# Block-sparse attention with an MLP mixer on one core: Q as whole rows, score products on four quarters of the array, V rows of 136 columns

## The chip, the core and the metric

The kernel runs on one core of one Trainium2 chip. A core has a matrix engine (TensorE, in the profile PE, with its weight loads as PEld), a vector engine (DVE), a scalar engine (ACT), GpSimd (POOL) and SyncE (SP), which here only issues DMAs. SBUF has 128 partitions; TensorE writes into PSUM, whose banks hold 2048 bytes in each partition. The metric is the time of one execution on the device in microseconds; lower is better.

## The reference

Two batches, eight heads, 768 queries of 64 numbers each. Every query sees the keys less than 16 positions away, and besides them 24 summary keys, one for each block of 32 keys.

```python
k_sum = k.reshape(B, H, nb, block, D).max(axis=3)
v_sum = v.reshape(B, H, nb, block, D).mean(axis=3)
mask_l = np.abs(pos[:, None] - pos[None, :]) < window
scores_s = scale * np.einsum('bhsd,bhnd->bhsn', q, k_sum) + np.log(block)
scores_all = np.concatenate([np.where(mask_l, scores_l, -1e9), scores_s], axis=-1)
a = np.exp(scores_all - scores_all.max(-1)); a = a / (a.sum(-1) + 1e-9)
attn = a @ np.concatenate([v, v_sum], axis=2)
...
u = x + tokenmix(x)               # x: attn, heads side by side, 512 columns
u = u + relu(u @ w_ch1) @ w_ch2   # 512 -> 1536 -> 512
out = u + relu(layernorm(u) @ moe2_w_ch1) @ moe2_w_ch2   # 512 -> 2048 -> 512
```

## The kernel before

The work has two parts. The attention goes pair by pair (two heads of one batch, eight pairs), and each pair in three **steps** of four windows of 64 queries: 24 steps, n = 0 to 23. Behind it, and partly beside it, stand the token mixing (`g1`, `g2`) and two large feed-forward layers, whose products are made in three parts from operands split into a high and a low half (`mm3`); the weights are loaded as 62 pieces and split on DVE and ACT (`dec`, `wh`, `wl`).

One step of the attention is a chain over the engines. `att_qk` makes the scores `sc` on PE: for each of four windows one product whose stationary side is a 128 x 128 piece of Q and whose moving side is 120 columns of K (96 neighbours and 24 summary keys). The 128 columns of the piece are the 64 queries of one head and the 64 queries of the other; since both heads' rows stand in the 128 partitions, the tile Q is filled in a pattern of blocks with zeros between, so that each query meets its own head's keys alone. `att_exp` reads the scores on DVE four times (`sn`, with the mask added and the row's extreme `mn` beside it), and ACT takes four exponentials `pr`. `att_tr` transposes the four `pr` on PE into `pt`, `att_evac` copies that to `PT` in SBUF (ACT, in every third step DVE), `att_av` multiplies with V in eight products of 64 columns of the array (`av`), `att_norm` divides on DVE (`rec`, `u`), and `att_hi` (ACT, `xh`) and `att_lo` (POOL, `xl`) split the result for the token mixing.

Per pair there are loads of K, Q (two DMAs of 64 partitions, in pieces of 512 bytes), V (two) and a transposed V (`VT`). `prep_k` and `copy_k` make the summary keys, `prep_v1` sums VT on POOL (for pair 0 on DVE, `Z`), `prep_v2` transposes Z on PE (`psv`) and ACT copies it into V four times. K and Q of three pairs fit at a time, V and VT of two.

The order of the work comes from the table `ORDER`: each event of step n or pair i gets a time (for `att_qk` it is n), `attention` sorts them and emits them, and a scheduler of the language then orders each engine's instructions. Scores lie in PSUM in the pool `ps_sc` with two buffers of one bank, so that the scores of step n can be written when the reads of step n-2 are done. Every DMA on SP waits until the DMA that was issued eight earlier has landed. Pair 0's Q is the one load that is issued from ACT's queue (`load_pair(0, nc.scalar)`). At the start, two memsets on DVE and four on POOL write the zeros of the three Q tiles, and 24 large products on PE (`warm`) run before the first load lands.

Of the kernel before, what the change touches and what calls it, by code (L numbers as in the profile page):

```python
# [26 lines left out]
NK = 96 + NB  # L27
ST = S // P
# [24 lines left out]
class Kern:  # L53
# [227 lines left out]
    def att_qk(self, n):  # L281
# [3 lines left out]
        ps = self.ps_sc.tile([P, 4, P], F32, tag="sc", name=f"sc{n}")  # L285
        for u in range(4):
            w = 4 * qd + u
            a = 184 * (w // 2) + 88 * (w % 2)
            nc.tensor.matmul(  # L289
                ps[:, u, :NK],  # L290
                Q[:, 64 + P * w : 64 + P * w + P],
                K.rearrange("p v c -> p (v c)")[:, a : a + NK],
                start=True,
                stop=True,
            )
        self.sc[n] = ps

    def att_exp(self, n):
# [7 lines left out]
        for u in range(4):  # L306
# [4 lines left out]
                ps[:, u, :NK],  # L311
# [26 lines left out]
    def att_av(self, n):  # L338
# [6 lines left out]
        for u in range(4):  # L345
            w = 4 * qd + u
            j = w % 2
            for r in range(2):
                nc.tensor.matmul(  # L349
                    ps[64 * j : 64 * j + 64, u // 2, 65 * r : 65 * r + 65],  # L350
                    pt[:, u * P + 64 * (r ^ j) : u * P + 64 * (r ^ j) + 64],
                    V[:, j, w // 2, 64 * r : 64 * r + 65],
                    start=True,
                    stop=True,
                )
# [264 lines left out]
    def run(self):  # L620
# [22 lines left out]
        self.ps_sc = actx.enter_context(tc.tile_pool(name="ps_sc", bufs=2, space=PSUM))  # L643
# [22 lines left out]
        for i in range(3):  # L666
# [183 lines left out]
```

## Time and profile before

| | |
|---|---|
| median of 3 runs | 613.52 us (613.23 to 614.16) |
| the profiled execution: its own time | 612.73 us |
| its span in the trace | 610.9 us |
| PE busy | 587.1 us (96%), 3368 instructions |
| DVE busy | 340.4 us (56%) |
| ACT busy | 208.5 us (34%) |
| mean granted clock of PE | 0.985 of full speed |

The span is the time from the first to the last instruction that the profiler recorded; the time of the same execution is 1.8 us longer, for what lies around the span. "Busy" is the time in which an engine executes anything. PE's busy time comes from records whose ends are modelled: a busy PE can be one that runs at half clock, which the row of the granted clock tells.

### The profile page before, as it was taken

Reading aid. Unit: us, or ns where it says so; the run is one execution under the profiler, and the core shown is the slowest. Engines: PE = TensorE matmul, PEld = TensorE weight load, DVE = VectorE, ACT = ScalarE, POOL = GpSimd, SP = SyncE. Lnnn points to the kernel's source line nnn. Section 1 sums busy time; section 2 is a strip of 40 time slices with the busy share of each in tenths; the row PEclk is TensorE's granted clock in tenths of the full one; section 3 lists DMA queues with packets and bytes.
Section 4 is the critical chain, followed back from the end, with each engine's and each line's share of the span. In section 5 each row is a group of like instructions: output and inputs, shape, how many; then the busy total and the mean of one; then the engine's idle time right before and its main releaser. Section 6 shows DMA issues by size and latency. Waiting matters only on the chain.

```text
span 610.9 us, 8732 instructions
## 1 busy us (share of the span) xinstructions
PE 587.1 (96%) x3368; PEld 521.6 (85%) x3368; DVE 340.4 (56%) x857; ACT 208.5 (34%) x458; POOL 45.8 (7%) x81
## 2 busy tenths in 40 slices
PE   7678899999999999999999999999999999999997
PEld 4567788879989898998989999999988999899896
DVE  5378778899567799787789951111143311111122
ACT  3677786535234345334334411111121110110110
POOL 2445433100000000000000000000000000000000
PEclk9779899999999999999999999999999999999999
DMA  9999862245423433344333200000000100000011
GB/s 213 290 228 234 212 156 75 75 133 169 142 67 113 132 89 90 102 134 125 117 104 104 69 1 1 0 1 0 1 17 36 53 0 1 1 0 1 0 53 52
DMA packets 27261, 51.78 MB, mean 85 GB/s; under 512 B 2130, under 2 KB 15186, under 8 KB 27220
## 3 DMA queue, kind: packets, MB, share of 16 engines
q1 hardware_dynamic: 26356, 50.80, 29.4%
q8 instruction: 26, 0.43, 0.3%
q10 hardware_dynamic: 864, 0.43, 0.3%
q14 instruction: 15, 0.12, 0.1%
HBM read 48.07 MB, written 3.15 MB: 84 GB/s over the span
## 4 chain that ended last, share of the span: by engine, by line
PE 88%; DVE 4%; DMA 3%; ACT 3%; issue 1%; POOL 1%; ACTq 0%; SPq 0%; DVEq 0%; POOLq 0%
PE sc L289 2%; PE av L349 2%; PE g L199 2%; PE g L198 1%; PE g L200 1%; DMA V<-in_v_dram 1%; DMA Q<-in_q_dram 1%; PE pt L326 1%; PE tx L510 1%; DVE dec L135 1%; PE tu L443 1%; ACT pr L319 1%; PE acc_('x', 2)_0_4643 L199 1%; PE acc_('x', 0)_0_3642 L199 1%; PE acc_('x', 0)_2_3644 L199 1%
## 5 line engine op out<-in xcount | busy, mean ns | idle before, releaser
L135 DVE SCALAR_TENSOR_TENSOR dec<-stage,dec 128x512 uint32<-128x512 uint32 x62 | 44.1, 712 | 0.8
L182 DVE TENSOR_TENSOR wl<-dec,wh 128x512 fp32r<-128x512 f32 x62 | 43.0, 696 | 1.2 <-DMA stage<-in_wts_dram 1.1
L131 DVE SCALAR_TENSOR_TENSOR dec<-stage,dec 128x512 uint32<-128x512 uint32 x62 | 42.9, 692 | 0.9
L113 ACT ACTIVATE dec<-stage 128x512 f32<-128x512 f32 x62 | 41.6, 673 | 4.7 <-DMA stage<-in_wts_dram 4.6
L175 ACT CAST wh<-dec 128x512 fp32r<-128x512 f32 x62 | 38.0, 616 | 12.7 <-DVE dec L135 12.5
L319 ACT ACTIVATE pr<-sn,mn 128x120 f32<-128x120 f32 x96 | 31.7, 385 | 7.6 <-DVE mn L309 7.4
L289 PE MATMUL sc<-K,Q 128*128 128x120 f32 x192 | 29.8, 304 | 1.5 <-DMA Q<-in_q_dram 1.0
L289 PEld LDWEIGHTS sc<-K,Q 128*128 128x128 f32 x192 | 26.9, 214 | 3.2 <-issue 1.4
L127 DVE TENSOR_SCALAR dec<-dec 128x512 f32<-128x512 f32 x62 | 26.5, 429 | 2.6 <-ACT dec L113 2.4
L129 DVE TENSOR_SCALAR dec<-dec 128x512 uint32<-128x512 uint32 x62 | 27.2, 439 | 0.8
L309 DVE CUSTOM_DVE_ANT_0 sn<-sc,mask 128x120 f32<-128x120 f32 x96 | 22.3, 275 | 8.8 <-PE sc L289 4.3
L326 PE MATMUL pt<-ident,pr 128*120 128x128 f32 x96 | 20.1, 294 | 6.7 <-ACT pr L319 2.8
L389 POOL TENSOR_TENSOR xl<-u,xh 128x256 fp32r<-128x256 f32 x24 | 19.7, 824 | 65.9 <-ACT xh L380 65.9
L349 PEld LDWEIGHTS av<-V,PT 121*64 121x64 f32 x384 | 16.2, 144 | 9.3 <-issue 5.8
L349 PE MATMUL av<-V,PT 121*64 121x65 f32 x384 | 19.8, 237 | 4.4 <-issue 3.8
L326 PEld LDWEIGHTS pt<-ident,pr 128*120 128x120 f32 x96 | 11.8, 142 | 10.0 <-ACT pr L319 5.0
L260 POOL TENSOR_TENSOR VT<-VT 128x384 f32<-128x384 f32 (+3 forms) x28 | 18.2, 650 | 1.6
L272 ACT ACTIVATE V<-psv 24x384 f32<-24x384 f32 x32 | 14.1, 476 | 4.9 <-PE psv L269 4.8
L199 PE MATMUL g<-xl,wh 128*128 128x256 f32 x48 | 14.5, 304 | 0.7 <-POOL xl L389 0.6
L198 PE MATMUL g<-xh,wh 128*128 128x256 f32 x48 | 14.0, 306 | 0.5 <-ACT xh L380 0.5
L200 PE MATMUL g<-xh,wl 128*128 128x256 f32 x48 | 14.0, 300 | 0.5 <-DVE wl L182 0.5
L485 DVE TENSOR_SCALAR xn<-u,mv,rs 128x128 f32<-128x128 f32 x48 | 13.9, 341 | 0.0
(3007 smaller groups left out, 1678.7 us busy)
## 6 DMA issues: line engine op xcount, KB each, us to landing
stage<-in_wts_dram SPq DMA_DIRECT2D x62, 512.0 KB, 3.5
V<-in_v_dram SPq DMA_DIRECT2D x16, 290.2 KB, 7.8
K<-in_k_dram SPq DMA_DIRECT2D x8, 480.0 KB, 8.5
VT<-in_vt_dram SPq DMA_DIRECT2D x8, 384.0 KB, 6.8
out_dram<-u SPq DMA_DIRECT2D x12, 256.0 KB, 2.0
Q<-in_q_dram SPq DMA_DIRECT2D x7, 224.0 KB, 7.9
Q<-in_q_dram SPq DMA_DIRECT2D x7, 192.0 KB, 6.9
mask<-in_mask_dram SPq DMA_DIRECT2D x1, 240.0 KB, 5.3
```

Source lines behind the costliest of these rows:

```text
L113: nc.scalar.activation(m, self.raw[n][:, :, 1].bitcast(F32), AF.Abs)
L127: nc.vector.tensor_scalar(m, m, MAG_LO, MAG_HI, op0=ALU.max, op1=ALU.min)
L129: nc.vector.tensor_scalar(mi, mi, 3, 0x3FFFFFF8, op0=ALU.logical_shift_left, op1=ALU.bitwise_and)
L131: nc.vector.scalar_tensor_tensor(mi, t[:, :, 1], 0xC0000000, mi, op0=ALU.bitwise_and, op1=ALU.bitwise_or)
L135: nc.vector.scalar_tensor_tensor(mi, t[:, :, 0], 29, mi, op0=ALU.logical_shift_right, op1=ALU.bitwise_or)
L175: self.nc.scalar.copy(self.slots[c if c < 16 else c - 16][0][:, s], x)
L182: self.nc.vector.tensor_tensor(wl[:, s], x, f32(wh[:, s]), op=ALU.subtract)
L199: nc.tensor.matmul(out, lhs[0], rhs[1], start=False, stop=False)
L289: nc.tensor.matmul(ps[:, u, :NK], Q[:, 64 + P * w : 64 + P * w + P], K.rearrange("p v c -> p (v c)")[:, a : a + NK], start=True, stop=True,)
L319: nc.scalar.activation(pr[:, u], sn[:, u], AF.Exp, bias=mn[:, u : u + 1], scale=-1.0)
L326: nc.tensor.transpose(ps[:NK, u * P : u * P + P], pr[:, u], self.ident)
L349: nc.tensor.matmul(ps[64 * j : 64 * j + 64, u // 2, 65 * r : 65 * r + 65], pt[:, u * P + 64 * (r ^ j) : u * P + 64 * (r ^ j) + 64], V[:, j ...
```

## The change

Q is kept as it comes: one tile of 128 x 768 (64 rows of each head), without zeros, filled by one DMA of whole rows of 3072 bytes. The six memsets and the padding on the host fall away. The scores of a window are now two products, one for each head r, each with a stationary side of 64 x 64 in the quarter of the array with rows 64r and columns 64(r^j), where j is the window's parity; a step has eight such products of 120 columns instead of four that fill the array. They are written to one PSUM tile `scores` of two banks, one for each j: even steps use one half of both banks, odd steps the other. `att_exp` reads it there. `att_av` emits its eight products in the order e, r, j instead of u, r, so that neighbours lie in different column halves. V's rows grow from 129 to 136 columns (3096 to 3264 bytes in a row of a DMA).

```diff
+VC = 136
...
-        qa, qb = self.q[b, p, 0:64], self.q[b, p, 64:128]
-        queue.dma_start(
-            Q[64:128, 128:1664].rearrange("p (n c) -> p n c", c=256)[:, :, 0:128],
-            qb[:, 64 : 64 + S].rearrange("p (n c) -> p n c", c=128),
-        )
-        queue.dma_start(
-            Q[0:64, :1664].rearrange("p (n c) -> p n c", c=128)[:, ::2],
-            qa.rearrange("p (n c) -> p n c", c=128),
-        )
+        queue.dma_start(Q, self.q[b, p])
...
-        ps = self.ps_sc.tile([P, 4, P], F32, tag="sc", name=f"sc{n}")
-        for u in range(4):
-            w = 4 * qd + u
-            a = 184 * (w // 2) + 88 * (w % 2)
-            nc.tensor.matmul(
-                ps[:, u, :NK],
-                Q[:, 64 + P * w : 64 + P * w + P],
-                K.rearrange("p v c -> p (v c)")[:, a : a + NK],
...
+        ps = self.scores[:, :, n % 2]
+        for e in range(2):
+            for r in range(2):
+                for j in range(2):
+                    w = 4 * qd + 2 * e + j
+                    a = 184 * (w // 2) + 88 * j
+                    rows, cols = slice(64 * r, 64 * r + 64), slice(64 * (r ^ j), 64 * (r ^ j) + 64)
+                    nc.tensor.matmul(
+                        ps[cols, j, e, :NK],
+                        Q[rows, 64 * w : 64 * w + 64],
+                        K.rearrange("p v c -> p (v c)")[rows, a : a + NK],
...
-                ps[:, u, :NK],
+                ps[:, u % 2, u // 2, :NK],
...
-        for u in range(4):
-            w = 4 * qd + u
-            j = w % 2
+        for e in range(2):
             for r in range(2):
...
+                for j in range(2):
+                    u = 2 * e + j
...
+        self.scores = ps_sc.tile([P, 2, 2, 2, P], F32, name="scores")
...
-        self.Q = [att.tile([P, 2 * S + P], F32, name=f"Q{i}") for i in range(3)]
+        self.Q = [att.tile([P, S], F32, name=f"Q{i}") for i in range(3)]
-        self.V = [att.tile([NK + 1, 2, 6, 129], F32, name=f"V{i}") for i in range(2)]
+        self.V = [att.tile([NK + 1, 2, 6, VC], F32, name=f"V{i}") for i in range(2)]
...
-        for i in range(3):
-            blocks = self.Q[i].rearrange("p (n c) -> p n c", c=P)
-            for rows, first in ((slice(0, 64), 1), (slice(64, P), 0)):
-                (nc.vector if i == 0 else nc.gpsimd).memset(blocks[rows, first::2], 0.0)
```

The scheduler orders the instructions anew. On PE, just behind the 24 `warm` products, the program of before begins with the scores of steps 0, 1 and 2 (`sc_186`, `sc_213`, `sc_236`):

```order
L289 MATMUL sc_186<-K_97,Q_94 128x120 [waits DMAHW1_49,DMAHW2_49,DMAHW0_49,Activation_49]
L289 MATMUL sc_186<-K_97,Q_94 128x120 x3
L289 MATMUL sc_213<-K_97,Q_94 128x120 x4
L269 MATMUL psv_218<-ident,Z_106 120x128 [waits DMAHW4_49,DVE_49,Pool_49]
L326 MATMUL pt_245<-ident,pr_204 120x128 [waits Activation_49] x2
L289 MATMUL sc_236<-K_97,Q_94 128x120 [waits DVE_49]
L289 MATMUL sc_236<-K_97,Q_94 128x120 x3
L326 MATMUL pt_245<-ident,pr_204 120x128 [waits Activation_49] x2
L349 MATMUL av_285<-V_102,PT_100 64x65 [waits DMAHW0_49,DMAHW6_49,Activation_49,Pool_49]
```

After the change all steps write the one tile `scores`:

```order
L285 MATMUL scores<-K_98,Q_95 64x120 [waits DMAHW1_49,DMAHW0_49,Activation_49]
L285 MATMUL scores<-K_98,Q_95 64x120 x7
L262 MATMUL psv_216<-ident,Z_107 120x128 [waits DMAHW3_49,DVE_49,Pool_49]
L322 MATMUL pt_246<-ident,pr_199 120x128 [waits Activation_49]
L285 MATMUL scores<-K_98,Q_95 64x120 [waits DVE_49]
L285 MATMUL scores<-K_98,Q_95 64x120 x7
L322 MATMUL pt_246<-ident,pr_199 120x128 [waits Activation_49] x3
L285 MATMUL scores<-K_98,Q_95 64x120 [waits DVE_49]
L285 MATMUL scores<-K_98,Q_95 64x120 x7
L345 MATMUL av_289<-V_103,PT_101 64x65 [waits DMAHW5_49,DMAHW7_49,Activation_49,Pool_49]
```

The scores of step 1 (the second group of `scores`) stood before without a wait, right behind those of step 0; now they wait for DVE, and stand behind the transpose `psv` and the first transpose of step 0. The product `av` of step 0 stands behind the scores of step 2 in both.

On ACT, the same place in the program: `pr_204` (before) and `pr_199` (after) are the exponentials of step 0, the next two `pr` those of steps 1 and 2, `V` the copies of `psv`, `PT` the copy of step 0's transposes.

```order
L244 COPY K_97<-ks_182 128x7x24 [waits DVE_49]
L319 ACTIVATE pr_204<-sn_202,mn_203 128x120 [waits DVE_49] x4
L272 ACTIVATE V_102<-psv_218 24x6x64 [waits PE_49]
L272 ACTIVATE V_102<-psv_218 24x6x64 x3
L319 ACTIVATE pr_227<-sn_225,mn_226 128x120 [waits DVE_49] x4
L319 ACTIVATE pr_259<-sn_257,mn_258 128x120 [waits DVE_49] x4
L336 COPY PT_100<-pt_245 120x512 [waits PE_49]
L244 COPY K_98<-ks_200 128x7x24 [waits DVE_49]
L380 CAST xh_112<-u 128x2x128 [waits DVE_49]
```

```order
L237 COPY K_98<-ks_175 128x7x24 [waits DVE_49]
L265 ACTIVATE V_103<-psv_216 24x6x64 [waits PE_49]
L315 ACTIVATE pr_199<-sn_197,mn_198 128x120 [waits DVE_49] x4
L265 ACTIVATE V_103<-psv_216 24x6x64 x3
L315 ACTIVATE pr_225<-sn_223,mn_224 128x120 [waits DVE_49] x4
L332 COPY PT_101<-pt_246 120x512 [waits PE_49]
L315 ACTIVATE pr_260<-sn_258,mn_259 128x120 [waits DVE_49] x4
L376 CAST xh_113<-u 128x2x128 [waits DVE_49]
L237 COPY K_99<-ks_195 128x7x24 [waits DVE_49]
```

The copy `PT` of step 0 stood behind twelve exponentials and four copies into V; now it stands behind eight and four. One copy into V has moved ahead of step 0's exponentials.

On SP, the loads of pair 1 (`K_98`, `Q_95` before; `K_99`, `Q_96` after) and what stands ahead of them:

```order
L228 DMA V_102<-in_v_dram 96x774
L684 DMA V_102<-in_guard_dram 1x1548 [waits DMAHW0_49]
L684 DMA V_103<-in_guard_dram 1x1548 [waits DMAHW1_49]
L208 DMA K_98<-in_k_dram 128x6x160 [waits DMAHW2_49]
L210 DMA Q_95<-in_q_dram 64x6x128 [waits DMAHW3_49]
L214 DMA Q_95<-in_q_dram 64x7x128 [waits DMAHW4_49]
L686 DMA gt<-in_g_dram 128x4 [waits DMAHW5_49]
L221 DMA VT_105<-in_vt_dram 128x768 [waits DMAHW6_49]
```

```order
L221 DMA V_103<-in_v_dram 96x816
L676 DMA V_103<-in_guard_dram 1x1632
L676 DMA V_104<-in_guard_dram 1x1632 [waits DMAHW0_49]
L209 DMA K_99<-in_k_dram 128x6x160 [waits DMAHW1_49]
L210 DMA Q_96<-in_q_dram 128x768 [waits DMAHW2_49]
L678 DMA gt<-in_g_dram 128x4 [waits DMAHW3_49]
L214 DMA VT_106<-in_vt_dram 128x768 [waits DMAHW4_49]
```

With one DMA less ahead of it, each load waits for a landing that lies one earlier in the row: the load of K of pair 1 waits on DMAHW1 instead of DMAHW2, and only one DMA of V's last row, instead of two, waits at all. Behind the last event of the attention the two programs stand in the same order on every engine.

## Rows read from the trace of the kernel before

**Rows 1.** The page, part 2: PE's busy share and granted clock in 40 slices.
```profile
PE   7678899999999999999999999999999999999997
...
PEclk9779899999999999999999999999999999999999
```

**Rows 2.** Busy time by stretch: columns stand in the first line.
```profile
core 0: us, PE busy (x) PEld busy (x) DVE busy (x) ACT busy (x) POOL busy (x), PEclk, DMA share, GB/s
9.80:31.30 21.50, 13.92 (x122) 12.28 (x123) 10.70 (x60) 14.88 (x43) 6.69 (x14) 0.84 1.08 270
31.30:82.00 50.70, 42.18 (x411) 36.26 (x410) 42.16 (x164) 37.46 (x98) 25.52 (x41) 0.90 0.93 226
82.00:113.00 31.00, 30.92 (x309) 26.38 (x310) 25.19 (x95) 21.89 (x61) 7.84 (x10) 1.00 0.34 96
113.00:165.00 52.00, 50.48 (x262) 44.34 (x261) 46.36 (x90) 23.81 (x44) 1.19 (x2) 1.00 0.44 138
...
15.34:22.17 6.83, 4.89 (x33) 4.80 (x34) 1.51 (x10) 3.65 (x12) 2.27 (x3) 0.50 1.06 287
...
225.00:611.00 386.00, 382.25 (x1942) 344.18 (x1940) 168.07 (x364) 86.42 (x169) 0.00 (x0) 1.00 0.14 44
```

**Rows 3.** The timeline of 0 to 20 us, all engines: start, length, instruction.
```profile
9.79 0.95 DVE L252 TENSOR_REDUCE Z<-VT 128x24 f32<-128x768 f32 x1 [3.47 <-DMA VT<-in_vt_dram]
9.79 2.02 PE L289 MATMUL sc<-K,Q 128*128 128x120 f32 x16 [0.98 <-DMA Q<-in_q_dram]
...
10.95 0.28 DVE L309 CUSTOM_DVE_ANT_0 sn<-sc,mask 128x120 f32<-128x120 f32 x1
...
11.28 1.26 ACT L319 ACTIVATE pr<-sn,mn 128x120 f32<-128x120 f32 x4 [4.59 <-DVE mn L309]
...
12.44 1.72 ACT L272 ACTIVATE V<-psv 24x384 f32<-24x384 f32 x4
...
14.18 2.39 ACT L319 ACTIVATE pr<-sn,mn 128x120 f32<-128x120 f32 x8
...
16.59 0.59 ACT L336 COPY PT<-pt 120x512 f32<-120x512 f32 x1
...
17.28 1.23 PE L349 MATMUL av<-V,PT 121*64 121x65 f32 x16 [3.83 <-issue]
...
19.77 0.72 POOL L389 TENSOR_TENSOR xl<-u,xh 128x256 fp32r<-128x256 f32 x1 [14.38 <-ACT xh L380]
```

**Rows 4.** Waits of DVE, 31.3 to 113 us: total, times, longest.
```profile
DVE rec L363 <- PE av L349: 4.2, 5, 1.1
DVE sn L309 <- PE sc L289: 2.9, 2, 2.4
```

**Rows 5.** Busy time by stretch, as above: two stretches of saturated DMA.
```profile
25.00:27.00 2.00, 1.90 (x24) 1.42 (x24) 1.36 (x11) 1.95 (x7) 1.12 (x5) 1.00 1.02 400
29.00:31.00 2.00, 0.46 (x4) 0.47 (x5) 0.00 (x0) 1.96 (x7) 0.00 (x0) 1.00 1.27 178
```

**Rows 6.** The chain in order of time, 0 to 108 us: start, length, step.
```profile
23.48 0.34 PE psv L269
...
43.12 1.77 PE sc L289 x8
...
94.55 0.88 PE sc L289 x8
...
95.77 0.38 PE av L349 x4
...
98.61 0.67 PE av L349 x16
...
100.36 0.44 PE pt L326 x4
```

**Rows 7.** The timeline of 82 to 89 us: one step's scores and reads.
```profile
84.10 1.05 PE L289 MATMUL sc<-K,Q 128*128 128x120 f32 x8
...
85.29 0.27 DVE L309 CUSTOM_DVE_ANT_0 sn<-sc,mask 128x120 f32<-128x120 f32 x1
```

More of the change, by code (lines that the diff above doesn't have):

```diff
@@ L284, in att_qk @@
         Q, K = self.Q[i % 3], self.K[i % 3]
-        ps = self.ps_sc.tile([P, 4, P], F32, tag="sc", name=f"sc{n}")
-        for u in range(4):
-            w = 4 * qd + u
-            a = 184 * (w // 2) + 88 * (w % 2)
-            nc.tensor.matmul(
-                ps[:, u, :NK],
-                Q[:, 64 + P * w : 64 + P * w + P],
-                K.rearrange("p v c -> p (v c)")[:, a : a + NK],
-                start=True,
-                stop=True,
-            )
+        ps = self.scores[:, :, n % 2]
[9 more added lines that the diff above has]
+                        K.rearrange("p v c -> p (v c)")[rows, a : a + NK],
+                        start=True,
+                        stop=True,
+                    )
         self.sc[n] = ps
@@ L344, in att_av @@
         self.av[n] = ps
-        for u in range(4):
-            w = 4 * qd + u
-            j = w % 2
+        for e in range(2):
             for r in range(2):
[L349 to L355, printed above, removed]
+                for j in range(2):
+                    u = 2 * e + j
+                    nc.tensor.matmul(
+                        ps[64 * j : 64 * j + 64, e, 65 * r : 65 * r + 65],
+                        pt[:, u * P + 64 * (r ^ j) : u * P + 64 * (r ^ j) + 64],
+                        V[:, j, 2 * qd + e, 64 * r : 64 * r + 65],
+                        start=True,
+                        stop=True,
+                    )
     def att_norm(self, n):
@@ L642, in run @@
         self.ps_mm = ctx.enter_context(tc.tile_pool(name="ps_mm", bufs=2, space=PSUM))
-        self.ps_sc = actx.enter_context(tc.tile_pool(name="ps_sc", bufs=2, space=PSUM))
+        ps_sc = actx.enter_context(tc.tile_pool(name="ps_sc", bufs=1, space=PSUM))
+        self.scores = ps_sc.tile([P, 2, 2, 2, P], F32, name="scores")
         self.ps_pt = actx.enter_context(tc.tile_pool(name="ps_pt", bufs=2, space=PSUM))
@@ L665, in run @@
         nc.gpsimd.memset(warm[1], 0.0)
-        for i in range(3):
-            blocks = self.Q[i].rearrange("p (n c) -> p n c", c=P)
-            for rows, first in ((slice(0, 64), 1), (slice(64, P), 0)):
-                (nc.vector if i == 0 else nc.gpsimd).memset(blocks[rows, first::2], 0.0)
-            if i == 0:
-                for t in self.Z:
-                    nc.gpsimd.memset(t, 0.0)
-                for t in self.V:
-                    nc.gpsimd.memset(t[0:NB, 0, :, 64:65], 1.0)
-                    nc.gpsimd.memset(t[96:NK, 1, :, 64:65], 1.0)
+        for t in self.Z:
+            nc.gpsimd.memset(t, 0.0)
+        for t in self.V:
+            nc.gpsimd.memset(t[0:NB, 0, :, 64:65], 1.0)
+            nc.gpsimd.memset(t[96:NK, 1, :, 64:65], 1.0)
         for t in self.PT:
@@ L792, in _layout @@
     t = lambda x: x.reshape(B, NPAIR, 2, S, D)
-    a["q"] = np.zeros((B, NPAIR, P, S + P), np.float32)
-    a["q"][..., 64 : 64 + S] = t(q).transpose(0, 1, 2, 4, 3).reshape(B, NPAIR, P, S)
+    a["q"] = t(q).transpose(0, 1, 2, 4, 3).reshape(B, NPAIR, P, S)
     a["vt"] = t(v).transpose(0, 1, 2, 4, 3).reshape(B, NPAIR, P, S)
@@ L800, in _layout @@
     vp[:, :, :, 16 : 16 + S] = t(v)
-    vw = np.ones((B, NPAIR, 2, 96, 6, 129), np.float32)
+    vw = np.ones((B, NPAIR, 2, 96, 6, VC), np.float32)
     for w in range(NW):
@@ L822, in _layout @@
     a["mask"] = _mask()
-    a["guard"] = np.zeros((1, 2, 6, 129), np.float32)
+    a["guard"] = np.zeros((1, 2, 6, VC), np.float32)
     a["guard"][..., 64] = EPS
```

## The prediction

> **What bounds the kernel now.** I read first the 40 slices of the page [rows 1]: PE stands at 9 tenths or more from slice 5 to the last but one, at full clock; only the first five slices (0 to 76 us) show gaps, and the lower clocks lie there too. Then busy time by stretch [rows 2], which cuts the attention into three regimes:
>
> - 9.8 to 31.3 us, the start: no engine is full (PE 13.92 and ACT 14.88 of 21.50), the DMA engines are (share 1.08). What counts is the chain of single waits.
> - 31.3 to 82 us: PE and DVE are both busy 42.2 of 50.7, ACT 37.5. They take turns at waiting.
> - 82 to 113 us: PE is busy 30.92 of 31.00. PE alone sets the end.
>
> Behind that, from 113 to 165 PE is busy 50.48 of 52.00, and from 225 to 611 it is 382.25 of 386.00. No edit touches those instructions, and their order is the same in both programs, so the time changes by as much as the attention ends earlier or later.
>
> **The first step of the chain.** In the timeline [rows 3] the scores of steps 0 and 1 (16 records) start at 9.79, the sums `Z` of VT at the same 9.79; the first read `sn` follows at 10.95, behind Z and its copy. ACT takes four exponentials (11.28), four copies into V (12.44), eight exponentials (14.18, steps 1 and 2), and only then, at 16.59, the copy `PT` of step 0 on which `av` (17.28) waits. From `av` hang `xl` on POOL (19.77), behind it POOL's sums for pair 1, and `psv` at 23.48 [rows 6]. So here ACT's order sets what comes later.
>
> **What the change costs and saves, part by part.**
>
> *ACT's order at the start.* PT of step 0 now stands behind eight exponentials instead of twelve. Eight took 2.39 [rows 3], so four are 1.20 us. Against it one copy into V, 1.72 / 4 = 0.43 us, now stands ahead of the first exponentials. It waits for `psv`, which waits for Z (done at 10.95), so it may push the exponentials back: between 0 and 0.6 us. Together the order gives -0.6 to -1.2; I take -0.9.
>
> *Q's load.* A stretch in which mostly Q's 512-byte pieces move shows 178 GB/s, one in which K, V and weights move 400, both at full DMA share [rows 5]. Q is 0.39 MB a pair: at 178 GB/s 2.2 us, at 400 1.0 us. So up to 1.2 us of DMA time per pair. Q of pair 0 stands ahead of the load of VT that releases Z at 9.79, and the DMA engines share the time between both, so not all arrives there: bounds 0 and -1.2. The K of pair 1 is also issued a landing earlier. I take -1.2 in all, since Z, the scores and the later loads of the start all stand behind the same full DMA engines. Behind 31.3 us I book nothing: no wait of DVE on a load stands in its list [rows 4], and the work of the three engines covers the loads; if that cover is not complete, what shows is a gain again, not a loss.
>
> Start: -0.9 - 1.2 = **-2.1** (from -0.5 to -2.5).
>
> *The scores on quarters.* Before, a step's scores are 8 records in 0.88 us, 0.110 each [rows 6]. Now there are 16 of the same 120 columns. No row shows 64 x 64. The nearest is `av`: 121 x 64, two column halves. There 16 records take 0.67 us and 4 take 0.38 [rows 6], which makes 0.29 / 12 = 0.024 a record and 0.28 fixed per visit. At the rate of the scores, 0.110 / 120 per column, a record of 65 columns would be 0.060, and 16 in a row 0.95. So `av` does run two halves or more side by side, and pays 0.28 for entering and leaving. Bounds for the new scores: four at once without any fixed part 0.44; one after another with it 16 x 0.110 + 0.28 = 2.04; two at once 0.88 + 0.28 = 1.16; four at once with the fixed part 0.44 + 0.28 = **0.72**. I take the last, because it is nearest to what `av` shows, where records of different quarters overlap: -0.16 us a step at full clock. At half clock (8 records in 1.77 [rows 6]) it is 0.88 + 0.28 to 0.56, that is -0.33 to -0.61.
>
> The Trainium skill, "TensorEngine Tiling (Array Packing)", Key Properties, says that a change of tiling mode drains the array, and that tiles operate independently; the program has such changes in 93 places instead of 51. The fixed 0.28 in [rows 6] agrees with a drain, and it is in the sum already.
>
> *One buffer pair instead of two buffers.* This is the loss. Both steps' halves share both banks, so the scores of step n+1 now wait for the reads of step n, where they waited for those of n-1 (the order at the start shows it: the second group of scores has a wait on DVE that it had not). [Rows 7] show a place where this bites: scores start at 84.10, and the last read of the step before starts at 85.29 and takes 0.27, so these scores would be 1.46 late. Behind them on PE stand transposes and an `av`, and DVE's next reads wait for them. The order has been made anew and puts other PE work ahead of many scores, so that most of the wait is filled. The reads of one step follow those of the step before mostly after 1 us or more, which covers a score block of 0.72. Bounds: 0, and 1.46 in each of the six steps of the PE-bound stretch, 8.8 us. I take +0.6 once between 31.3 and 82, and +0.3 in all between 82 and 113.
>
> *31.3 to 82.* DVE waits for scores only twice, 2.9 us, the longer 2.4 us [rows 4]; that is a score block at half clock on the chain at 43.12 [rows 6]. It gets 0.5 shorter (the middle of 0.33 and 0.61). With the +0.6: **+0.1** (from -1.5 to +2).
>
> *82 to 113.* Six steps of 0.16 = -1.0, plus 0.3: **-0.7** (from -1.5 to +8).
>
> *The rest.* The order of `av`'s products: `av` overlaps already; bounds -0.1 and +0.1 a step, I take 0. V's 5.4% more bytes are 31 KB a pair, 0.08 us at 400 GB/s and 0.17 at 178, hidden where loads land early, 0. The memsets of Q (DVE and POOL) lie ahead of 9.79, while the first loads are on their way, 0.
>
> **Sum.** -2.1 + 0.1 - 0.7 = **-2.7 us**. The profiled execution took 612.73 (span 610.9 and 1.8 around it) and would take 610.0. The median of the runs shown, 613.52, lies 0.8 above it; I take the change from there: **610.8**. Its own range is 608 to 612.3.
>
> **The rivals.**
>
> *More at the start (R1).* From 15.34 to 22.17 PE runs at half clock (0.50) and is busy 4.89 of 6.83 [rows 2]. It follows a stretch in which PE idles (3.83 us ahead of 17.28 [rows 3]). If `av` comes 2 us earlier, this gap is halved, and the slow stretch may not come or come shorter: half of the 4.89, some 2.4 us, comes back on top of the sum, or up to 4 with the half-clock blocks near 43 us. For it: the gap is the longest of the start. Against it: scores and `av` still wait for each other, and three gaps remain. Time 605 to 608; from there down to 603 at best.
>
> *No change (R2).* DVE and ACT carry 42.2 and 37.5 of 50.7 us in the middle stretch [rows 2], with the same number of instructions as before. What the start gains can run out against them: a chain that is 2 us early meets a DVE that has 8.5 us of idle time in all, 7 of them behind PE [rows 4]. Then only the -0.7 is left, and the new waits take it back: 612.5 to 614.5.
>
> *Quarters that do not run four at once (R4).* Two row halves that write one bank may take turns. Then a step's scores take 1.16, +0.28 a step: +1.7 in the PE-bound stretch and +0.3 of waits, some +1.1 in the middle, -1.8 at the start: +1.3, or 614.8 (613.5 to 616). One after another (2.04, +1.16 a step) costs 7 in the last stretch alone: above 619. `av`'s overlap is between column halves that share their rows; no row of before shows two row halves at work. The Trainium skill, "TensorEngine Tiling (Array Packing)", Gotcha 1: PSUM Pressure, says that different row tiles cannot access one PSUM bank at the same time; here heads 0 and 1 of one parity write one bank, in different partitions. By that rule it is this rival.
>
> *Slower by the new wait (R3).* Place: 82 to 113, where PE has 0.08 us of idle time in all [rows 2], so that each wait of PE that nothing fills is lost. Price up to 1.46 a step [rows 7], six steps, 8.8 us. It decides against the change when the mean added wait in these six steps passes (2.7 + 0.3) / 6 = 0.5 us; at 1 us it gives 6.0 - 3.0 = +3.0, about 616.5. Against it: DVE idles 5.8 of 31.0 there, and PE has products of the token mixing to put between.
>
> **How the numbers follow.** 0.2% (1.2 us) is about what a measurement of this kernel can tell from no change: faster is below 612.3, slower above 614.7. The forecast 0.48 (faster). R1 0.20 (faster). R2 0.12: same 0.10, faster 0.02. R4 0.11: same 0.05, slower 0.06. R3 0.09, slower. That gives faster 0.70, same 0.15, slower 0.15. The range 604 to 616 leaves out the lowest part of R1 (0.04), the upper half of R3 (0.05) and the one-after-another case of R4 (0.02).
>
> **What the profile after would show.** Right: `av` of step 0 near 15.2 instead of 17.28; a score block of 16 records in some 0.7 us at full clock; `psv` of pair 1 near 21.4; PE busy without gaps from about 80; the attention's end near 110. Wrong: blocks of 1.1 or 2.0 us (R4); PE waits on DVE's reads `mn` of 0.5 us a step and more between 80 and 113 (R3); PE's granted clock at full through 15 to 22 us (R1); DVE without idle time between 30 and 80 and the end of the attention still at 113 (R2). What would make the forecast wrong above all is the order that the new waits give to the scheduler: it moves products of the token mixing and of three steps against each other, and I costed that at the 0.9 us of waits alone.

## The result, and the profile after

The changed kernel takes 604.88 us (median of 4 runs, 603.89 to 606.72) against 613.38 us (4 runs, 613.01 to 614.16): a ratio of 0.9867, with a 95% interval of 0.9843 to 0.9892. That is 8.5 us less, where 2.7 were forecast. The profiled execution took 604.47 us, with a span of 602.7 us against 610.9.

The 40 slices of the page of the changed kernel, PE's busy share and its granted clock:

```profile
PE   7777999999999999999999999999999999999997
...
PEclk9679899999999999999999999999999999999999
```

PE reaches 9 tenths in slice 4 instead of slice 5 [rows 1]. But the row of the clock shows 9, 6, 7, 9, 8 in the first five slices, where it showed 9, 7, 7, 9, 8: PE runs no faster at the start, and the kernel is faster nevertheless.

The timeline of the start, all engines (start, length, instruction):

```profile
7.73 0.95 DVE L245 TENSOR_REDUCE Z<-VT 128x24 f32<-128x768 f32 x1 [1.51 <-DMA VT<-in_vt_dram]
...
9.39 0.64 PE L285 MATMUL scores<-K,Q 64*64 64x120 f32 x16
...
10.10 0.28 DVE L305 CUSTOM_DVE_ANT_0 sn<-scores,mask 128x120 f32<-128x120 f32 x1 [1.20 <-PE scores L285]
...
10.71 1.23 ACT L315 ACTIVATE pr<-sn,mn 128x120 f32<-128x120 f32 x4
...
11.85 1.35 ACT L265 ACTIVATE V<-psv 24x384 f32<-24x384 f32 x3
...
13.06 0.92 PE L285 MATMUL scores<-K,Q 64*64 64x120 f32 x16 [0.55 <-DVE mn L305]
13.22 1.25 ACT L315 ACTIVATE pr<-sn,mn 128x120 f32<-128x120 f32 x4
...
14.50 0.59 ACT L332 COPY PT<-pt 120x512 f32<-120x512 f32 x1
...
15.18 1.23 PE L345 MATMUL av<-V,PT 121*64 121x65 f32 x16 [1.20 <-issue]
...
17.68 0.72 POOL L385 TENSOR_TENSOR xl<-u,xh 128x256 fp32r<-128x256 f32 x1 [15.65 <-ACT xh L376]
...
18.37 1.08 PE L285 MATMUL scores<-K,Q 64*64 64x120 f32 x16 [1.96 <-ACT K L237]
```

Against [rows 3]: the sums Z start at 7.73 instead of 9.79, the first `av` at 15.18 instead of 17.28, `xl` at 17.68 instead of 19.77. A step's scores are 16 records in 0.64 us at full clock; those at 13.06, across the fall of the clock, take 0.92, and those at 18.37, at half clock, 1.08. In the chain of work that ended last, later in the attention, one block is 0.57 us, where it was 0.88 [rows 6]:

```profile
78.27 0.57 PE scores L285 x16
...
92.51 0.57 PE scores L285 x16
```

**Three accounts.** From one product of the token mixing on (the 2500th PE record from the end) both programs do the same in the same order; it starts at 114.2 us before and at 105.5 after, and from there to the end of the span both take 497 us (496.8 and 497.2). So the whole difference lies ahead of that point. What PE does up to it falls into three parts: **idle** time; **work**, which is its busy time as it would be at full clock; and **lost** to the clock, which is half of its busy time in stretches at a clock of 0.50. The stretches of the changed kernel, columns as in [rows 2] (the last row is the stretch just ahead of the first fall of the clock):

```profile
0.00:105.50 105.50, 91.12 (x1061) 67.39 (x1062) 81.19 (x322) 76.38 (x204) 43.56 (x77) 0.87 0.68 214
13.28:26.94 13.66, 9.19 (x106) 6.50 (x99) 5.46 (x30) 8.85 (x25) 5.93 (x13) 0.50 0.94 300
37.18:44.00 6.82, 5.99 (x35) 4.58 (x35) 5.64 (x25) 5.44 (x15) 4.42 (x9) 0.50 1.01 355
57.66:64.48 6.82, 5.75 (x61) 4.22 (x57) 6.82 (x28) 5.49 (x14) 3.81 (x6) 0.50 1.04 324
9.40:13.28 3.88, 2.47 (x46) 1.60 (x49) 1.80 (x16) 2.92 (x9) 0.00 (x0) 1.00 1.10 346
```

And of the kernel before, where the first stretch of half clock, 15.34 to 22.17, stands in [rows 2]:

```profile
0.00:114.20 114.20, 95.38 (x869) 79.87 (x870) 82.11 (x324) 76.80 (x205) 45.49 (x81) 0.93 0.79 198
39.23:46.06 6.83, 5.37 (x25) 4.97 (x25) 4.46 (x22) 5.55 (x16) 2.65 (x4) 0.50 1.05 259
63.13:66.54 3.41, 3.41 (x29) 2.74 (x27) 3.05 (x15) 0.93 (x4) 0.00 (x0) 0.50 0.97 276
```

Before: idle 114.2 - 95.38 = 18.8; busy at half clock 4.89 + 5.37 + 3.41 = 13.67, so 6.8 lost; work 95.38 - 6.84 = 88.5. After: idle 105.5 - 91.12 = 14.4; busy at half clock 9.19 + 5.99 + 5.75 = 20.93, so 10.5 lost; work 91.1 - 10.5 = 80.6. The change saves 7.9 us of work and 4.4 us of idle time, and gives 3.6 us back to the clock. The same account of all kernels that ran, with their medians and their ratios to the kernel before (the account is that of each one's profiled execution, whose own time stands beside the median, up to the same product):

| kernel | median us | ratio, 95% interval | profiled us | up to the product | idle | work | lost |
|---|---|---|---|---|---|---|---|
| before | 613.4 | | 612.73 | 114.2 | 18.8 | 88.5 | 6.8 |
| changed | 604.88 | 0.9843 to 0.9892 | 604.47 | 105.5 | 14.4 | 80.6 | 10.5 |
| e1_twice | 603.35 | 0.9809 to 0.9857 | 603.64 | 104.6 | 11.5 | 88.4 | 4.8 |
| e2_wait | 617.60 | 1.0023 to 1.0095 | 619.98 | 121.2 | 17.9 | 89.0 | 14.2 |
| e3_pieces | 610.83 | 0.9931 to 0.9969 | 611.00 | 112.1 | 19.3 | 80.6 | 12.1 |
| e4_diag | 610.83 | 0.9939 to 0.9968 | 611.79 | 112.3 | 14.3 | 88.2 | 9.8 |
| e5_pieces_same | 605.05 | 0.9851 to 0.9880 | 604.80 | 105.8 | 14.5 | 80.8 | 10.4 |
| e6_two_dmas | 610.53 | 0.9933 to 0.9968 | 608.73 | 109.8 | 17.3 | 79.6 | 13.0 |
| e7_diag_same | 607.98 | 0.9902 to 0.9957 | 606.88 | 107.9 | 13.3 | 90.1 | 4.6 |
| e8_fill | 603.03 | 0.9819 to 0.9848 | 602.57 | 103.7 | 14.0 | 85.4 | 4.2 |
| e9_avorder | 603.97 | 0.9822 to 0.9862 | 604.31 | 105.4 | 15.0 | 80.6 | 9.8 |
| e10_v129 | 604.01 | 0.9828 to 0.9874 | 603.58 | 104.6 | 15.3 | 79.7 | 9.6 |
| e11_fill_psv | 605.27 | 0.9840 to 0.9912 | 604.03 | 105.0 | 12.5 | 86.3 | 6.2 |
| e12_before_fill | 615.96 | 1.0027 to 1.0059 | 613.68 | 115.0 | 15.7 | 93.4 | 6.0 |

### The profile page after: what moved, and what is told of

It reads as the page before. It is cut to its first block, busy times and chain, and to the rows that moved or that the text cites. A ratio compares the mean times of both kernels' runs of the same rounds, so it can differ in the third digit from the quotient of the medians.

```text
span 602.7 us, 9099 instructions
## 1 busy us (share of the span) xinstructions
PE 583.0 (97%) x3560; PEld 509.3 (85%) x3560; DVE 339.3 (56%) x855; ACT 208.2 (35%) x458; POOL 44.2 (7%) x77
## 4 chain that ended last, share of the span: by engine, by line
PE 90%; DVE 3%; ACT 3%; POOL 2%; issue 1%; POOLq 0%; DVEq 0%; ACTq 0%
PE scores L285 2%; PE g L199 2%; PE g L201 2%; PE g L200 2%; PE av L345 1%; PE pt L322 1%; PE warm_ps L685 1%; POOL VT L253 1%; PE tx L506 1%; POOL xl L385 1%; ACT V L265 1%; DVE sn L305 1%; PE acc_('x', 2)_0_4702 L200 1%; PE acc_('x', 0)_0_3701 L200 1%; PE acc_('x', 0)_2_3703 L200 1%
## 5 line engine op out<-in xcount | busy, mean ns | idle before, releaser
L128 DVE TENSOR_SCALAR dec<-dec 128x512 f32<-128x512 f32 x62 | 27.8, 450 | 1.5 <-ACT dec L114 1.4
L305 DVE CUSTOM_DVE_ANT_0 sn<-scores,mask 128x120 f32<-128x120 f32 x96 | 21.6, 277 | 8.6 <-PE scores L285 7.2
L285 PE MATMUL scores<-K,Q 64*64 64x120 f32 x384 | 18.5, 309 | 3.6 <-ACT K L237 2.0
L253 POOL TENSOR_TENSOR VT<-VT 128x384 f32<-128x384 f32 (+3 forms) x28 | 19.3, 690 | 1.6
L285 PEld LDWEIGHTS scores<-K,Q 64*64 64x64 f32 x384 | 11.8, 150 | 8.7 <-DVE mn L305 2.3
L265 ACT ACTIVATE V<-psv 24x384 f32<-24x384 f32 x32 | 14.5, 478 | 7.6 <-PE psv L262 7.2
L200 PE MATMUL g<-xl,wh 128*128 128x256 f32 x48 | 14.3, 303 | 0.5 <-POOL xl L385 0.5
```

Source lines behind the costliest of these rows:

```text
L128: nc.vector.tensor_scalar(m, m, MAG_LO, MAG_HI, op0=ALU.max, op1=ALU.min)
L200: nc.tensor.matmul(out, lhs[0], rhs[1], start=False, stop=False)
L285: nc.tensor.matmul(ps[cols, j, e, :NK], Q[rows, 64 * w : 64 * w + 64], K.rearrange("p v c -> p (v c)")[rows, a : a + NK], start=True, stop ...
L305: nc.vector.tensor_tensor_reduce(sn[:, u], ps[:, u % 2, u // 2, :NK], self.mask[:, mv], scale=-SCALE, scalar=3e38, op0=ALU.add, op1=ALU.mi ...
```

## The experiments

The theory at the outset, A: the gain is PE's time for the scores, on the path of nearly all steps. Its rivals: B, the loads and the start bring it; C, the order that the scheduler makes around the new wait brings it; R3 of the prediction, the wait costs and the cheaper products hide it.

**e1_twice: each score product made twice.**

```diff
-        for e in range(2):
+        for e in (0, 0, 1, 1):
```

> Every score product of the changed kernel is made twice (the second overwrites the first with the same numbers); all else as in the changed kernel. In the changed kernel a step's scores take 0.64 us at full clock; 16 records more, four at once, are about 0.44 us more, so a step then costs about what it cost before the change (0.88 to 1.1). Theory A (the gain of 8.5 us is TensorE's time for the scores, on the path of nearly all 24 steps): 24 x 0.44 = 10.6 us at most, some of it in idle time, so 610 to 615 us, most of the gain lost. Theory B (the gain comes from the earlier loads and the new order at the start and in the middle, the scores counting in the last six steps only): 6 x 0.44 = 2.6, about 607.5 us.

Measured: 603.35 us, not slower than the changed kernel. A block of scores, and the stretch up to the product, columns as above:

```profile
8.84 1.05 PE L285 MATMUL scores<-K,Q 64*64 64x120 f32 x32
```

```profile
0.00:104.60 104.60, 93.15 (x1444) 73.37 (x1445) 79.52 (x322) 76.00 (x204) 42.29 (x76) 0.95 0.69 216
```

The work is back at 88.4 us, that of the kernel before, and the end does not move: the 7.8 us of work come back as 5.7 us less lost to the clock and 2.9 us less idle time. The mean clock of this run is 0.991, that of the changed kernel 0.977. So PE's work can't be costed without its clock, and from here the three accounts are read apart. But this run does not keep all else as the expectation had it: the scheduler put the instructions of every engine in another order. On DVE the sums `ks` for the K of pair 1 start at 13.19 instead of 17.00, and PE starts the scores of step 3 at 15.75 instead of 18.37, where they wait for K in the changed kernel. Two things differ here, the work and the order, so this run does not decide between the theories; e7_diag_same, below, has a block of nearly this length in the unchanged order.

**e2_wait: the kernel before, its scores in the shared banks.**

```diff
-        ps = self.ps_sc.tile([P, 4, P], F32, tag="sc", name=f"sc{n}")
+        ps = self.scores[:, :, n % 2]
...
-                ps[:, u, :NK],
+                ps[:, u % 2, u // 2, :NK],
```

> The kernel before, with Q's zeros, loads and full-array products, but its scores written to the one tile of two banks that both steps share: the new wait alone. Theory R3 (the wait costs, the cheap products hide it): each step's scores start after the reads of the step before, up to 1.46 us a step where PE has no idle time; 616 to 622 us. Theory C (the order made anew around this wait is itself what brings the gain): 606 to 610 us. Theory A: the wait is filled by other PE work, 612.5 to 615 us.

Measured: 617.60 us, 3.8 us slower than the kernel before on the same chip (613.8).

```profile
0.00:121.20 121.20, 103.31 (x869) 86.61 (x870) 85.51 (x324) 76.81 (x204) 45.20 (x81) 0.86 0.74 186
```

The order that the scheduler makes around the wait brings no gain here, so C falls as far as this run goes; its order is neither that of the kernel before nor that of the changed kernel. The wait has the price that R3 gave it a place for, but not by R3's mechanism: idle time is 121.2 - 103.31 = 17.9 us, less than before, work is nearly the same, and lost to the clock are 14.2 instead of 6.8 us (a mean clock of 0.86 instead of 0.93 up to the product). The account is that of an execution of 619.98 us. The seven runs lie between 613.30 us, at a mean clock of 0.989, and 620.18 us, at 0.971: the fastest shows no price at all, and the price goes with a clock that differs from run to run.

**e3_pieces and e6_two_dmas: Q by two DMAs again, in pieces of 512 bytes and as whole rows.** Each of the two has the other's order on every engine.

```diff
-        queue.dma_start(Q, self.q[b, p])
+        for h in (slice(64, 128), slice(0, 64)):
+            queue.dma_start(Q[h].rearrange("p (n c) -> p n c", c=P), self.q[b, p, h, :, 0:P])   # e3_pieces
+            queue.dma_start(Q[h], self.q[b, p, h])                                              # e6_two_dmas
```

> The changed kernel with Q loaded by two DMAs of 64 partitions in pieces of 512 bytes again (from a padded array in DRAM, into the same tile without zeros): the load's part alone. My step put 1.2 us on the load, all at the start: av of step 0 back from 15.2 to about 16.4 us and 606.1 us. Theory B (loads are most of the gain): 610 us and more. Theory A: what the start loses is kept or lost to waits later, 604.5 to 606.5 us.

> The changed kernel with Q loaded as whole rows by two DMAs of 64 partitions each; every engine's order is that of e3_pieces, so that against e3 only the size of the pieces differs, and against the changed kernel the number of DMAs and the order that follows from it. Theory D: as e3, 609 to 612 us. Theory L: as the changed kernel, 604 to 606 us.

Measured: 610.83 and 610.53 us: the size of the pieces makes no difference, and the second DMA per pair costs 5.7 us. With one DMA more the scheduler puts PE's instructions in another order. That the order costs the time, and not the DMA itself, is inferred: after `Z` at the start, which waits 2.3 us for VT, none of the computing engines waits for a load up to the product. Where e6_two_dmas loses is one place. Up to the 3000th PE record from the end it is 0.7 us behind the changed kernel, forty records later 3.9, and it ends 4.3 us behind (its profiled execution, 608.73 us, is the fastest of five). The stretch up to the product and the one at that place in e6_two_dmas, and the latter in the changed kernel:

```profile
0.00:109.80 109.80, 92.53 (x1060) 69.24 (x1061) 83.68 (x322) 76.96 (x204) 42.82 (x76) 0.84 0.75 206
64.48:69.32 4.84, 4.84 (x43) 4.12 (x45) 3.39 (x14) 4.75 (x13) 1.93 (x2) 0.50 0.50 116
```

```profile
64.48:69.32 4.84, 4.58 (x66) 3.39 (x66) 3.60 (x15) 4.79 (x14) 2.39 (x4) 1.00 0.88 271
```

From 64.48 to 69.32 e6_two_dmas runs at half clock, the changed kernel at full. The low clock of e6_two_dmas lasts there from 55.66 to 69.32, that of the changed kernel from 57.66 to 64.48. Behind it PE stands 1.00 us for an `xl`:

```profile
72.81 0.38 PE L200 MATMUL g<-xl,wh 128*128 128x256 f32 x1 [1.00 <-POOL xl L386]
```

**e5_pieces_same: one DMA, pieces of 512 bytes, every engine in the order of the changed kernel.**

```diff
-        queue.dma_start(Q, self.q[b, p])
+        queue.dma_start(Q.rearrange("p (n c) -> p n c", c=P), self.q[b, p, :, :, 0:P])
```

> The changed kernel with Q loaded in pieces of 512 bytes, but by one DMA as in the changed kernel: every engine has its instructions in the same order as the changed kernel, so that this is the size of the pieces alone. In e3_pieces the steps up to 14 kept the times of the changed kernel (the reads of step 14 ended at 66.98 instead of 67.59 us) and no engine waited for a load; it lost 5 us between 67 and 77 us, where its PE order is another one. Theory D (the size of the pieces costs next to nothing, e3 lost by its order and by the clock): 604 to 606 us. Theory L (the pieces cost what e3 lost): 609 to 611 us.

Measured: 605.05 us; theory D holds. The timeline of its start:

```profile
8.51 0.95 DVE L245 TENSOR_REDUCE Z<-VT 128x24 f32<-128x768 f32 x1 [2.42 <-DMA VT<-in_vt_dram]
...
15.43 1.22 PE L345 MATMUL av<-V,PT 121*64 121x65 f32 x16 [1.40 <-issue]
```

VT lands 0.8 us later than in the changed kernel (8.41 against 7.63), `av` of step 0 comes 0.25 us later (15.18), and the end 0.3 us. But the 0.25 us are not the load's. The first scores start 0.25 us later too (9.64 against 9.39), in both kernels right behind the last `warm` product, and VT has landed before; from there on the two traces agree within 0.1 us up to the product. In the other kernels that load Q as whole rows by one DMA, VT lands between 7.14 and 8.16. So the whole rows bring nothing that the start or the time shows. B falls as far as it means the size of the pieces.

**e4_diag and e7_diag_same: two quarters at once.** Both use only the two quarters on the diagonal; e4_diag gives each step a bank of its own again and emits r innermost, e7_diag_same keeps the shared banks and with them, on every engine, the order of the changed kernel.

```diff
-                    rows, cols = slice(64 * r, 64 * r + 64), slice(64 * (r ^ j), 64 * (r ^ j) + 64)
+                    rows = cols = slice(64 * r, 64 * r + 64)
...
-                        pt[:, u * P + 64 * (r ^ j) : u * P + 64 * (r ^ j) + 64],
+                        pt[:, u * P + 64 * r : u * P + 64 * r + 64],
```

> The changed kernel with its eight score products on the two diagonal quarters alone (rows of head r, columns 64r), two at once, each step in a bank of its own as before the change, so that scores wait for the reads of step n-2 again; av takes its stationary columns accordingly. Theory A (TensorE's time for the scores is the gain, the wait is cheap): a step's scores take 0.88 and some 0.2 for the change of mode, about 1.05 to 1.16 instead of 0.64, so most of the gain is lost: 609 to 615 us. Theory of the wait (the shared banks cost much of a larger gain): free of the wait it keeps 604 us or beats it.

> The changed kernel with the eight score products on the two diagonal quarters alone, two at once, in the shared banks; every engine's order is that of the changed kernel. A step's scores take about 1.2 us at full clock (as in e4_diag) instead of 0.64. Theory A (TensorE's time for the scores is on the path, part by part): the attention's work on PE grows by about 7.7 us (88.4 in e4_diag against 80.8 us), and the end moves by that less what falls into idle time and what the clock gives back: 607 to 613 us. Theory B (scores hardly on the path): 604 to 606 us.

Measured: 610.83 and 607.98 us. A block of scores in e7_diag_same, and its stretch up to the product:

```profile
8.46 1.09 PE L285 MATMUL scores<-K,Q 64*64 64x120 f32 x16
```

```profile
0.00:107.90 107.90, 94.65 (x1060) 74.20 (x1061) 81.24 (x322) 76.88 (x204) 42.45 (x77) 0.95 0.66 209
```

1.09 us instead of 0.64 a block: two at once are 0.88 + 0.21, four at once 0.44 + 0.20. With nothing else changed the work grows by 9.5 us; 5.9 us come back from the clock and 1.1 from idle time, which leaves 2.5 us in the profiled execution, the fastest of four. Between the medians lie 3.1 us. That the four quarters run at once is therefore worth about 3 us here, though it saves 9.5 us of PE's work.

Since the order is the same, the two traces also show where these 3 us are lost. Counted from the first score product, which starts at 8.46 here and at 9.39 in the changed kernel, the scores of step 16 and of step 22, here and then in the changed kernel:

```profile
70.24 1.09 PE L285 MATMUL scores<-K,Q 64*64 64x120 f32 x16
...
91.11 1.09 PE L285 MATMUL scores<-K,Q 64*64 64x120 f32 x16
```

```profile
71.18 0.64 PE L285 MATMUL scores<-K,Q 64*64 64x120 f32 x16
...
89.53 0.64 PE L285 MATMUL scores<-K,Q 64*64 64x120 f32 x16
```

Step 16 stands at 61.78 and 61.79. Ahead of it the difference moves between -0.3 and 0.9 us, so that sixteen steps with the longer block cost nothing by then: the waits and the clock take them up. Step 22 stands at 82.65 and 80.14, 2.5 us apart, and the product of the token mixing 3.4 us. So the shorter block counts from step 16 on alone, where PE is busy 34.32 of 34.32 us up to the product in the changed kernel, at full clock. Theory A holds for these last steps and not for all 24.

e1_twice makes its scores in a block of nearly the same length (1.05 us), has 1.7 us less work in all, and is 4.6 us faster than e7_diag_same. The rest of these 4.6 us goes with its other order.

The quarters do run at once: the sixteen further records of e1_twice take 1.05 - 0.64 = 0.41 us, 0.026 each, where a record takes 0.110 by itself [rows 6]. It agrees with what the Trainium skill, "TensorEngine Tiling (Array Packing)", says under Key Properties, that tiles operate independently. Under Gotcha 1: PSUM Pressure of the same page the Trainium skill says that different row tiles cannot access one PSUM bank at the same time; here two row halves wrote one bank, in different partitions, and the 16 records took 0.64 us, little more than a third of the 1.76 that they would take one after another at the 0.110 of [rows 6]. The measurement decides: in different partitions they did not take turns.

e4_diag, with no wait on the step before, has the idle time of the changed kernel (14.3) and loses 5.2 us more than e7_diag_same to the clock (9.8 against 4.6). It differs in its order too, so this is no measure of the wait alone.

**e8_fill and e12_before_fill: 12 products more between 10 and 18 us,** on operands that are ready there and into a bank that nobody reads; in the changed kernel and in the kernel before.

```diff
+    def fill(self, x, k):
+        for _ in range(k):
+            self.nc.tensor.matmul(self.wps[:, : x.shape[-1]], self.ident[: x.shape[0]], x, start=True, stop=True)
...
+        for at, x, k in (
+            (1.36, lambda: self.Z[0], 3),
+            (2.15, lambda: self.prs[0][:, 3], 2),
+            (3.1, lambda: self.prs[1][:, 3], 4),
+            (3.66, lambda: self.PT[0][:NK], 2),
+            (4.01, lambda: self.PT[0][:NK], 1),
+        ):
+            put(at, lambda x=x, k=k: self.fill(x(), k))
```

> The changed kernel with 12 products more between 10 and 18 us, on operands that are there at that time and into a bank that nobody reads, so that PE has less idle time ahead of its first stretch at half clock (13.28 to 26.94 us). Theory K (the change costs clock: PE's busy time at half clock rose from 13.7 to 20.9 us, which costs 3.6 us more than before, because cheaper scores leave PE more idle): the stretch does not come or comes shorter and later, and 3 to 5 us are won: 600 to 602 us, the mean clock up from 0.977. Rival (the clock is lowered by something else, or the fill delays real work): same clock, 604.5 to 608 us.

> The kernel before with the same 12 fill products between 10 and 18 us. Its half-clock stretch 15.34 to 22.17 follows a gap of 3.83 us on PE, of which the fill covers about half. Theory K (PE's gaps at the start bring the low clock, whatever the scores are): the stretch comes later or shorter, 610 to 612.5 us. Rival (fill helps only the changed kernel, or the changed order takes it back): 613 to 616 us.

Measured: 603.03 us for the changed kernel with the fill. Its interval, 0.9819 to 0.9848, lies below that of e5_pieces_same, which has the order and the time of the changed kernel (0.9851 to 0.9880). The stretch up to the product and that of the fill in e8_fill, and the latter in the changed kernel:

```profile
0.00:103.70 103.70, 89.66 (x1085) 66.30 (x1086) 80.88 (x322) 76.07 (x204) 42.29 (x77) 0.95 0.71 218
9.40:18.40 9.00, 7.88 (x93) 5.55 (x93) 4.16 (x27) 6.58 (x19) 0.72 (x2) 1.00 1.07 318
```

```profile
9.40:18.40 9.00, 4.43 (x74) 3.04 (x73) 4.17 (x27) 6.58 (x19) 0.72 (x2) 0.72 1.08 319
```

Between 9.4 and 18.4 us PE is busy 7.88 of 9.00 us instead of 4.43, and the clock stays at 1.00 instead of 0.72; it falls first at 33.9. The sum up to the product: work +4.8, lost -6.3, idle -0.3. The expectation was 3 to 5 us, the gain 1.9. Up to 18.4 us the order is that of the changed kernel but for the fill; behind that the scheduler changed it on PE, DVE, ACT and POOL, so that the clock of the start is the fill's doing, while the 1.9 us are the fill's and the new order's together. In the kernel before the same fill brings nothing: 615.96 us, slower by 2.4. There the half-clock stretch at 15.34 is gone as well, but what is lost to the clock falls only from 6.8 to 6.0 us (the last of its later stretches is twice as long), idle time falls by 3.1 us, and the work grows by 4.9. Its order differs from that of the kernel before too. The profiled execution of e12_before_fill took 613.68 us, the fastest of its eight, so its account, 0.8 us in all, explains less than the median shows.

**e11_fill_psv: e8_fill with `psv` later.** In e8_fill PE stands longest here:

```profile
35.34 0.47 PE L262 MATMUL psv<-ident,Z 128*120 128x128 f32 x1 [3.04 <-POOL Z L256]
```

```diff
-    "vput": -0.15
+    "vput": 0.4
```

> e8_fill with the transposes psv of VT's sums put 0.55 of a step later in the table of times, because in e8_fill PE stood 3.0 us at 32.3 to 35.3 behind a psv that waited for POOL, with products behind it that were ready, and the clock fell at 33.9. Theory (idle time in that place costs twice, by itself and by the clock): 599 to 602 us. Rival (the later psv delays V, and the order around it is worse): 603 to 607 us.

Measured: 605.27 us (603.03 without this edit). The idle time is 1.6 us less, but lost to the clock are 2.0 and work 0.9 us more. The rival holds.

**e9_avorder and e10_v129: the order of av's products and V's rows as before.**

```diff
-            for r in range(2):
-                for j in range(2):
+            for j in range(2):          # e9_avorder
+                for r in range(2):
...
-VC = 136
+VC = 129                                # e10_v129
```

> The changed kernel with the products of av in the order e, j, r of the kernel before; the scheduler moves some transposes and scores of steps 5 to 9 by a place or two on PE, all else as in the changed kernel. My step booked 0 for this order: 604 to 606 us, and av blocks of the same length (16 records in 0.67 us at full clock). If neighbours in different halves matter: av blocks 0.1 us longer or more, 24 steps, 607 us and more.

> The changed kernel with V rows of 129 columns (3096 bytes) again; some places on PE, ACT and SP move. My step booked 0 for the bytes, hidden: 604 to 606 us if the order does nothing. What the small moves of order do by themselves shows here too: by e6_two_dmas, where a changed order cost 5.7 us, up to 610 us.

Measured: 603.97 and 604.01 us. Neither edit brings anything; without either the kernel is, within what the intervals tell, the same. A block of `av` takes 0.73 us in e9_avorder and 0.69 in the changed kernel at full clock.

## Why the prediction was right, and where its sizes were wrong

The direction and the range held (604.88 in 604 to 616), close to the lower end. The likeliest case's own range, 608 to 612.3, did not hold, and the number lies just below the 605 to 608 of R1, whose cause did not occur. That the range held at all is in part luck: its lower end was there for a clock that would stay up, and the gain came from elsewhere.

- **The start, -2.1: right in size, its parts wrong.** `av` -2.10, `xl` -2.09, `psv` of pair 1 at 21.56 instead of 23.48. On ACT `PT` starts 2.09 us earlier, and the starts ahead of it divide this. The first read `sn` starts at 10.10 instead of 10.95, 0.85 earlier; step 0's exponentials follow it 0.28 us later than before, with a copy into V now ahead of them; three copies into V behind them instead of four save 0.37, and four exponentials instead of eight 1.13. So ACT's order brings 1.2 us, where 0.9 was booked. For the load, booked at 1.2, at most the 0.85 is left, and none of it is the size of its pieces (e5_pieces_same); it was not taken apart from the missing memsets and the new order on SP.
- **The score block, 0.72: too long.** It measures 0.57 in the chain and 0.64 in the timeline, so a visit costs 0.13 to 0.20 beside its products, not the 0.28 taken over from `av`. A step saves 0.31 in the chain (0.88 before) and 0.41 in the timeline (1.05 before [rows 7]), not 0.16. R4 did not occur; with two quarters at once the kernel still takes 607.98 us, not R4's 613.5 to 616.
- **82 to 113, -0.7: the place was right, the size wrong.** With the end of step 17's reads as the border (80.86 before, 77.01 after) the changed kernel wins 4.9 us from there to the product, where the term's bounds ended at -1.5. The busy time of the scores alone in this stretch, before, changed and e7_diag_same (columns PE, PEld, DVE, then the clock and DMA):

```profile
80.86:114.20 33.34, 6.75 (x48) 6.21 (x48) 5.63 (x24) 1.00 0.38 105
```

```profile
77.01:105.50 28.49, 3.85 (x96) 2.47 (x96) 5.53 (x24) 1.00 0.27 91
```

```profile
76.92:107.90 30.98, 6.53 (x96) 5.15 (x96) 5.56 (x24) 1.00 0.25 79
```

  Six steps save 2.9 us, forecast was 1.0. By e7_diag_same, which needs 2.5 us more for the same stretch, the scores' saving shows there in full. The rest of the 4.9 us was booked at nothing or at a loss: PE's idle time falls from 0.7 us to none, where +0.3 of waits was forecast, and the records of `av` in this stretch are busy 5.83 us (140 of them) instead of 7.36 (144).
- **31.3 to 82, +0.1: the order had no term.** Between the start's 2.1 us and that border the changed kernel wins another 1.75 us; the bounds ended at -1.5. From its first scores the changed kernel takes 67.62 us to the border, and e7_diag_same, with the same order and longer blocks, 68.46, so that the scores are less than half of the 1.75. e6_two_dmas, with the same blocks in another order, takes 71.61, more than the kernel before (71.07). The prediction named the order as what would make it wrong above all, and costed it at the 0.9 us of waits alone.
- **R1: its clock went the other way.** It said that a shorter gap ahead of `av` may keep the clock up. The gap did shrink, from 3.83 to 1.20 us, and the low clock lasted twice as long (13.28 to 26.94 instead of 15.34 to 22.17). That it also began earlier says little: in e9_avorder and e10_v129, whose start has the same order, it began at 15.2 (and lasted 13.7 and 10.2 us). Nor does the share of idle time just ahead of it explain the difference: from 9.4 to 13.28 PE was busy 2.47 of 3.88 us, and before, from 9.80 to 15.34, 3.64 of 5.54, about two thirds in both. With more work at the start and the order of the changed kernel there, the clock falls later: at 18.19 in e7_diag_same and at 33.9 in e8_fill. Why the low stretch is longer in the changed kernel than in the one before stays open.
- **The new wait, +0.9: the place was wrong.** In the changed kernel PE waits for reads of the step before only at the start, as the list of its waits from 9.4 to 31.3 shows; from 31 to 100 us none is in the list:

```profile
PE scores L285 <- DVE mn L305: 1.7, 2, 1.1
```

  In the kernel before, the wait and the order that comes with it cost 3.8 us in the median (e2_wait), and the account puts that on the clock.
- **The rest, 0: right for the time** (e9_avorder, e10_v129; the memsets were not tried apart).

What brought the 8.5 us is shown in part. Four quarters at once instead of two bring 3.1 us, with every order the same. The kernel before had neither: its four products fill the array, in a block (1.05 us) of nearly the length of that with two quarters (1.09), so that 3.1 us is near what the shorter block is worth in this order, not measured as such, since no run puts the products of the kernel before into the changed order. One DMA for Q instead of two brings 5.7 us, by the order on the engines as far as can be told, since the size of the pieces changes nothing. That the two add up was not tried: no kernel undoes both and nothing else. Why the order of the one DMA is better is shown for one place only, the low clock from 64.48 to 69.32 and the wait behind it; that it is better in general, or would be in another build, stays open.

## What to carry to other kernels

Where PE's work is made cheaper in a stretch full of waits, read three accounts up to a common point: idle time, work at full clock, and what half clock takes; here 9.5 us of work were worth about 3 us. Count such a saving where the engine is the bound, at the length that the block has there, and ahead of that expect the waits and the clock to take it up. And where a scheduler orders the program, its order is a term of the sum: compare two variants with the same order before putting a difference on the thing that was edited. Here the size of a DMA's pieces looked like 6 us and was nothing, and score products made twice looked free, where a block of the same length in the unchanged order cost 3 us.

## What the runs showed of the hardware that was not expected

- Products on four quarters, two of them in the same PSUM bank but in other partitions, run at once: 16 records in 0.64 us, and 32 in 1.05 (e1_twice), 0.026 us for each further one, where one record of the whole array takes 0.110.
- More work can leave PE less time at half clock: with the same order and 9.5 us more work up to the product, the granted clock was half for 10.2 us instead of 27.3 (e7_diag_same against the changed kernel).
- Q by one DMA in pieces of 512 bytes or in rows of 3072 makes no difference to the time (605.05 and 604.88 us).
